# Two-pair partition moves, 64x64 tiles, 512-token FFN tiles and a shallower load queue in a fused attention and FFN kernel

## The chip, the cores and the metric

The kernel runs on one core of one Trainium2 chip. The metric is device time in microseconds (us), lower is better. The kernel before takes 254.39 us (median of 3 runs, 254.19 to 254.92). The span of a profile is about 1.8 us shorter than the time of the same run.

Engines are called as in the profile: PE (TensorE matmuls), PEld (its weight loads), DVE (VectorE), ACT (ScalarE), POOL (GpSimd, which issues the loads; before the change pair 0's q and k come through SP instead), SP (the sync engine, which issues stores and, after the change, moves; SPq in the profile is its queue). A matmul that runs at half clock is called cold here, one at full clock warm.

## The reference, cut to what matters

```
q, k, v: (8, 8, 576, 64) f32         # batch, heads, sequence, head size
chunks of 64 tokens; in each chunk and head:
    attn = softmax(q k^T / 8);  out = attn v
x = out, as (4608 tokens, 512)
result = ((x w1) * (x w2)) w3 w_out  # w1, w2: 512x1024; w3: 1024x1024; w_out: 1024x512
```

## The kernel before: the parts that matter here

The work is cut into 18 *pairs* of 256 tokens. A string lists every step in program order; each engine takes its own steps from it strictly in that order. For pair p:

- `q k v` load (POOL queue; casts f32 to bf16). `T p.s` transposes q or k blockwise (DVE). `S` computes scores (PE), `E` exponentials (ACT), `P` attention times v (PE), `N` divides (DVE), `X` transposes into xt (DVE).
- `A p.j`, `B p.j` are FFN matmuls with w1, w2 (PE), `C` copies A's result out of PSUM (ACT), `M` multiplies (DVE). `O` multiplies by w3 w_out (PE), `Y` copies (ACT) and stores (SP). `V W Z` form w3 w_out once. `D` is filler on zeros that keeps PE busy.

```
qk_t[p] = io.tile([P, 2, H, 2 * D], bf, tag="qk", bufs=6, name="qk")      # six pairs of q, k
vbuf = [consts.tile([P, 2, H, VW], bf, ...) for i in range(7)]            # seven pairs of v

def do_S(p):                       # 64 matmuls, K = 32 rows, accumulated over e
    for h in range(H):
        for e in range(2):
            for i in range(NB):    # NB = 4 blocks of 32 partitions
                mm(s_t[p][half[i % 2], i // 2, h * CH:(h + 1) * CH],
                   lhsT=qkT[blk[i], 1, e, h, :], rhs=qkT[blk[i], 0, e, h, :], start=(e == 0), stop=(e == 1))
def mm_ab(p, j, which):            # FFN: 256 tokens per matmul
    for i in range(2):
        for ki in range(KO):
            mm(ps_t[p, j][:, which, i * PT:(i + 1) * PT], lhsT=w[:, ki, ...], rhs=xt[:, ki, p * PT:(p + 1) * PT], ...)
...
S9 N8.0 O5 E9 X8.0 N8.1 X8.1 T11.0 A6.1 T11.1 Y5 B6.1 C6.1 ... P9 l16 M6.3 S10    # one pair's steps; l = q, k, v
```

All PSUM results share a ring of four buffers: a step that writes PSUM waits for the reader of the result four steps back.

The softmax here doesn't subtract the row's maximum and nothing guards it: scores larger than these inputs give would overflow.

Of the kernel before, what the change touches and what calls it, by code (L numbers as in the profile page):

```python
# [356 lines left out]
```

## Time and profile before

| Reading | Value | View |
|---|---|---|
| PE busy | 234.9 of 252.7 us (93%) | page, part 1 |
| One pair in steady state | 12.0 us | timeline of PE |
| of it A and B (64 matmuls of 256 columns) | 7.08 us, 110.6 ns each | timeline |
| O (16 of 512 columns) | 3.45 us, 215.6 ns each | timeline |
| P and S (64 small matmuls each) | 0.62 and 0.64 us, 9.9 ns each | timeline |
| DVE waiting for q, k loads | 3.5 us | waits |

The slices of the page: the span in 40 parts; each digit is the busy share in tenths (PEclk: the granted clock).

```profile
PE   1389999999899999999999999999999999999993
...
PEclk9999999999999999999999999999999999999999
DMA  7999999999999999999953020202021120102022
```

PE is full from 20 us to the end, so the kernel is bound by PE's own work. The DMA engines are full only for the first half.

The timeline of PE in steady state; the columns are start and duration in us, engine, line, operation, out<-in, the part of the array used (rows*columns), the shape of the moving operand, count. Durations overlap because matmuls are pipelined, so costs are read from start to start.

```profile
140.11 0.70 PE L88 MATMUL pv<-vbuf,e 64*32 64x65 bf16 x64
140.73 0.70 PE L88 MATMUL s_ps<-qkT 32*64 32x64 bf16 x64
141.57 3.61 PE L88 MATMUL o_ps<-w3o,ab 128*128 128x512 bf16 x16
145.02 7.15 PE L88 MATMUL ab_ps<-xt,w 128*128 128x256 bf16 x64
152.10 0.70 PE L88 MATMUL pv<-vbuf,e 64*32 64x65 bf16 x64
```

From 140.11 to 152.10 is one pair. O starts 0.20 us later than S's 0.64 us would allow: the chain of waits shows that it waits for the multiply of the last A, B (its PSUM buffer).

### The profile page before, as it was taken

The page shows a single profiled execution, that of the slowest core. Times are in us where ns is not written, and L with a number is a line of the kernel's source. Part 1 is how long each engine was busy: PE and PEld are TensorE (multiplying, and loading weights), DVE is VectorE, ACT ScalarE, POOL GpSimd, SP SyncE. Part 2 cuts the span into 40 slices and gives each one's busy share as a digit, 9 for nine tenths or more (in the row PEclk, how much of TensorE's full clock was granted, in tenths as well). Part 3 has the DMA queues.
Part 4 walks back from the last instruction along what each step waited for, and adds up shares of the span by engine and source line. Part 5 has one row for each costly group of instructions (what it writes and reads, how often), then busy time and mean ns, then how long its engine had stood idle before and what let it go on. Part 6 is the DMA issues. An engine that isn't in the chain of part 4 may idle for free.

```text
span 252.7 us, 8382 instructions
## 1 busy us (share of the span) xinstructions
PE 234.9 (93%) x3841; PEld 170.5 (67%) x3841; DVE 156.4 (62%) x233; ACT 86.3 (34%) x116; POOL 82.9 (33%) x110
## 2 busy tenths in 40 slices
PE   1389999999899999999999999999999999999993
PEld 1237878854555577866868686868686868678662
DVE  1665999699996457486665758584945445432230
ACT  3312424432433343333334243343334332323321
POOL 8756975657984567654020000000000000000000
PEclk9999999999999999999999999999999999999999
DMA  7999999999999999999953020202021120102022
GB/s 177 182 184 177 182 175 202 196 184 167 175 170 214 244 227 182 199 167 148 187 38 92 3 83 4 86 3 86 5 81 44 46 81 5 64 22 84 0 86 83
DMA packets 89763, 29.90 MB, mean 118 GB/s; under 512 B 73728, under 2 KB 85248, under 8 KB 89728
## 3 DMA queue, kind: packets, MB, share of 16 engines
q0 software_dynamic: 82592, 18.88, 80.4%
q1 hardware_dynamic: 7136, 10.49, 11.8%
q8 instruction: 30, 0.49, 0.7%
q14 instruction: 5, 0.04, 0.0%
HBM read 38.80 MB, written 9.44 MB: 191 GB/s over the span
## 4 chain that ended last, share of the span: by engine, by line
PE 65%; DMA 14%; DVE 10%; POOL 4%; ACT 3%; issue 3%; DVEq 0%; POOLq 0%
PE ab_ps L88 39%; PE o_ps L88 25%; DMA w<-in_moe_w_dram 4%; DVE ab L249 4%; DMA qk<-in_q_dram 4%; DMA qk<-in_k_dram 3%; DVE w3T L290 3%; DMA vbuf<-in_v_dram 3%; ACT a_sb L244 3%; POOL w L91 1%; DVE qkT L168 1%; POOL vbuf L91 1%; POOL qk L91 1%; POOL wo L91 1%; DVE xt L213 1%
## 5 line engine op out<-in xcount | busy, mean ns | idle before, releaser
L88 PE MATMUL ab_ps<-xt,w 128*128 128x256 bf16 x1136 | 128.0, 273 | 1.3 <-DVE xt L213 1.3
L88 PEld LDWEIGHTS <-w 128*128 128x128 bf16 x1152 | 112.3, 98 | 19.4 <-DVE xt L213 2.4
L249 DVE TENSOR_TENSOR ab<-a_sb,ab_ps 128x512 bf16<-128x512 f32 x71 | 48.3, 682 | 71.6 <-ACT a_sb L244 71.6
L244 ACT COPY a_sb<-ab_ps 128x512 f32<-128x512 f32 x71 | 41.6, 586 | 79.3 <-PE ab_ps L88 79.3
L88 PE MATMUL o_ps<-w3o,ab 128*128 128x512 bf16 (+1 forms) x296 | 65.3, 373 | 2.7 <-ACT o_sb L276 1.1
L88 PEld LDWEIGHTS <-ab 128*128 128x128 bf16 x296 | 28.7, 97 | 33.3 <-issue 1.6
L168 DVE STREAM_TRANSPOSE qkT<-qk 128x1024 bf16<-128x1024 bf16 x36 | 45.1, 1287 | 8.5 <-ACT qk L133 5.1
L91 POOL DMA_DIRECT2D vbuf<-in_v_dram x40 | 33.9, 852 | 31.3 <-PE pv L88 16.3
L283 ACT COPY o_sb<-o_ps 128x1024 f32<-128x1024 f32 x17 | 17.2, 1014 | 45.9 <-PE o_ps L88 43.2
L213 DVE STREAM_TRANSPOSE xt<-xn 128x512 bf16<-128x512 bf16 x36 | 25.6, 712 | 1.2
L209 DVE TENSOR_TENSOR xn<-pv,rc 128x512 bf16<-128x512 f32 x36 | 24.9, 692 | 1.2
L91 POOL DMA_DIRECT2D qk<-in_q_dram x23 | 18.1, 793 | 6.8 <-DMA qk<-in_k_dram 2.4
L184 ACT ACTIVATE e<-s_ps 128x1024 bf16<-128x1024 f32 x16 | 16.4, 1025 | 8.7 <-PE s_ps L88 8.4
...
L88 PEld LDWEIGHTS <-qkT 32*64 32x64 bf16 x1152 | 11.4, 111 | 10.6 <-DVE qkT L168 9.6
L88 PE MATMUL w_ps<-wo,w3T 128*128 128x512 bf16 x64 | 14.2, 379 | 0.0
L88 PEld LDWEIGHTS <-e 64*32 64x32 bf16 x1152 | 10.1, 90 | 5.5 <-issue 3.6
L88 PE MATMUL pv<-vbuf,e 64*32 64x65 bf16 x1152 | 12.7, 197 | 1.1 <-ACT e L184 1.1
L91 POOL DMA_DIRECT2D w<-in_moe_w_dram x16 | 11.1, 697 | 5.4 <-DMA wo<-in_moe_w_out_dram 3.0
L88 PE MATMUL s_ps<-qkT 32*64 32x64 bf16 x1024 | 11.3, 193 | 0.0
L88 PEld LDWEIGHTS <-w3T 128*128 128x128 bf16 x64 | 6.2, 98 | 7.1
L290 DVE STREAM_TRANSPOSE w3T<-w 128x1024 bf16<-128x1024 bf16 x8 | 9.6, 1211 | 0.9 <-DMA w<-in_moe_w_dram 0.9
...
## 6 DMA issues: line engine op xcount, KB each, us to landing
...
```

Of the source, the lines that this page charges most:

```text
L88: return inorder(nc.tensor.matmul(*a, **kw))
L91: return inorder(nc.gpsimd.dma_start(dst, src))
L168: inorder(nc.vector.transpose(qkT_t[p][:, s].rearrange("p e h (y t) -> p h t e y", t=2), qk_t[p][:, s].rearrange("p h (t e y) -> p h t e y ...
L184: inorder(nc.scalar.activation(e_t[p][:].rearrange("p u h q -> p u (h q)"), s_t.pop(p)[:], Exp, scale=scale, bias=0.0))
L209: inorder(nc.vector.tensor_mul(xn_t[p, u][:], pv[:, :, :, 0:D], rc.to_broadcast([P, 2, 4, D])))
L213: inorder(nc.vector.transpose(xt[:, :, t0:t0 + UT].rearrange("p o (m y) -> p m o y", y=BL), xn_t.pop((p, u))[:].rearrange("p r (c n) (z o) ...
L244: inorder(nc.scalar.copy(a_t[p, j][:], ps_t[p, j][:, 0, :]))
L249: inorder(nc.vector.tensor_mul(ab_t[p][:, 2 * j:2 * j + 2, :].rearrange("p j t -> p (j t)"), a_t.pop((p, j))[:], ps_t.pop((p, j))[:, 1, :]))
L283: inorder(nc.scalar.copy(o_sb[:], ps_t.pop(p)[:]))
L290: inorder(nc.vector.transpose(w3T_t[f][:].rearrange("p k (f y) -> p f k y", y=BL), w3[:, NB * f:NB * (f + 1), :].rearrange("p f (k x) -> p ...
```

## The change

From pair 8 on, q, k and x of *two pairs* at a time are moved between partitions by SBUF-to-SBUF DMAs (`G`, `H`, issued from SP). Then the contraction of S is 64 rows instead of twice 32, S and P run in 64x64 tiles with 32 matmuls each instead of 64, and the FFN takes 512 tokens per matmul instead of 256. To make room, and to leave the DMA engines free, loads are held: two buffers of q, k (two pairs ahead) and three of v. The order of all steps is new.

```
-    vbuf = [... for i in range(7)]
+    vbuf = [... for i in range(3)]
-            qk_t[p] = io.tile(..., tag="qk", bufs=6, ...)
+            qk_t[p] = io.tile(..., tag="qk", bufs=2, ...)
-            if p == 0:   # pair 0: f32 load on SP and a cast on ACT
-                ...
+    def do_G(g, a):                       # q, k of two pairs: 4 moves of 128 KB for each a = 0, 1
+        for i in (2 * a, 2 * a + 1):
+            for e in range(2):
+                move(qkm_t[g][blk[2 * a + e], i % 2], qkT_t[g][blk[i], e])
     def do_S(p):
+            if p < 8: (as before) else:
+                for i in (0, 3, 1, 2):
+                    mm(s_t[p][half[i % 2], i // 2, ...],
+                       lhsT=qkm_t[g][half[i // 2], i % 2, m, 1, h, :],
+                       rhs=qkm_t[g][half[i // 2], i % 2, m, 0, h, :], start=True, stop=True)
+    def do_H(g, a): ...                   # x of two pairs: 4 moves of 64 KB for each a
     do_P, do_X, do_A, do_B, do_M: likewise, two forms (p < 8 and p >= 8)
     do_O of the last pair: three PSUM tiles instead of one
+    do_Q: the store of O, apart from its copy Y
ORDER (start, and around pairs 8 to 12):
-l0 q1 i0 k1 v1 i1 i2 l2 i3 l3 l4 o h0 h1 l5 D0.0.16.64 ...
+q0 k0 v0 q1 k1 v1 i0 D0.0.104.64 T0.0 T0.1 q2 k2 v2 i1 i2 i3 S0 ...
-N6.1 X6.1 T9.0 T9.1 O3 ... P7 l14 M4.3 S8 N7.0 O4 ... T10.0 A5.0 T10.1 ... P8 l15 M6.0 S9 ... T11.0 ...
+T8.1 M4.2 T9.0 P6 v9 q10 k10 Y1 S7 T9.1 ... G4.0 ... O2 M4.3 N6.1 G4.1 X6.1 T10.0 P7 v10 q11 k11 ... O3 ...
+S8 Y3 A5.1 E8 B5.1 Q3 O4 ... T11.0 P8 v11 q12 k12 ... S9 ... A6.1 T12.0 B6.1 C6.1 M6.0 P9 v12 q13 k13 ...
-... A17.3 ... M17.3 O17 Y17
+... A16.7 ... M16.7 O16 O17 Y16 Q16 Y17 Q17
```

More of the change, by code (lines that the diff above doesn't have):

```diff
@@ L9 @@
 ORDER = """
-l0 q1 i0 k1 v1 i1 i2 l2 i3 l3 l4 o h0 h1 l5 D0.0.16.64 T0.0 T0.1 l6 S0 T1.0 E0 P0 D0.1.4.512 T1.1 l7
-N0.0 S1 D1.0.5.512 X0.0 N0.1 X0.1 A0.0 E1 B0.0 C0.0 P1 M0.0 A0.1 N1.0 X1.0 B0.1 C0.1 N1.1 A0.2 X1.1
-B0.2 C0.2 M0.1 A1.0 T2.0 B1.0 C1.0 M0.2 A1.1 T2.1 l8 B1.1 C1.1 M1.0 S2 M1.1 A0.3 E2 T3.0 B0.3 C0.3
-P2 M0.3 A1.2 N2.0 X2.0 B1.2 C1.2 N2.1 A1.3 X2.1 B1.3 C1.3 M1.2 A2.0 T3.1 l9 B2.0 C2.0 M1.3 S3 T4.0
-A2.1 E3 M2.0 B2.1 T4.1 C2.1 P3 l10 M2.1 A2.2 N3.0 B2.2 C2.2 X3.0 A2.3 N3.1 B2.3 X3.1 C2.3 M2.2 S4
@@ L15 @@
-M2.3 A3.0 E4 B3.0 C3.0 A3.1 M3.0 B3.1 C3.1 V0 A3.2 M3.1 B3.2 C3.2 V1 A3.3 M3.2 B3.3 C3.3 V2 W0 M3.3
-V3 T5.0 W1 Z0 V4 V5 T5.1 W2 Z1 V6 V7 T6.0 P4 l11 Z2 S5 T6.1 W3 E5 N4.0 X4.0 N4.1 X4.1 T7.0 A4.0 Z3
-B4.0 T7.1 C4.0 P5 l12 M4.0 S6 N5.0 O0 E6 X5.0 N5.1 X5.1 T8.0 O1 Y0 T8.1 P6 l13 Y1 S7 N6.0 O2 E7 X6.0
-N6.1 X6.1 T9.0 T9.1 O3 Y2 A4.1 Y3 B4.1 C4.1 A4.2 M4.1 B4.2 C4.2 A4.3 M4.2 B4.3 C4.3 P7 l14 M4.3 S8
-N7.0 O4 E8 X7.0 N7.1 X7.1 T10.0 A5.0 T10.1 Y4 B5.0 C5.0 A5.1 M5.0 B5.1 C5.1 A5.2 M5.1 B5.2 C5.2 A5.3
@@ L20 @@
-M5.2 B5.3 C5.3 A6.0 M5.3 B6.0 C6.0 P8 l15 M6.0 S9 N8.0 O5 E9 X8.0 N8.1 X8.1 T11.0 A6.1 T11.1 Y5 B6.1
-C6.1 A6.2 M6.1 B6.2 C6.2 A6.3 M6.2 B6.3 C6.3 P9 l16 M6.3 S10 N9.0 O6 E10 X9.0 N9.1 X9.1 T12.0 A7.0
-T12.1 Y6 B7.0 C7.0 A7.1 M7.0 B7.1 C7.1 A7.2 M7.1 B7.2 C7.2 A7.3 M7.2 B7.3 C7.3 P10 l17 M7.3 S11
-N10.0 O7 E11 X10.0 N10.1 X10.1 T13.0 A8.0 T13.1 Y7 B8.0 C8.0 A8.1 M8.0 B8.1 C8.1 A8.2 M8.1 B8.2 C8.2
-A8.3 M8.2 B8.3 C8.3 P11 M8.3 S12 N11.0 O8 E12 X11.0 N11.1 X11.1 T14.0 A9.0 T14.1 Y8 B9.0 C9.0 A9.1
@@ L25 @@
-M9.0 B9.1 C9.1 A9.2 M9.1 B9.2 C9.2 A9.3 M9.2 B9.3 C9.3 P12 M9.3 S13 N12.0 O9 E13 X12.0 N12.1 X12.1
-T15.0 A10.0 T15.1 Y9 B10.0 C10.0 A10.1 M10.0 B10.1 C10.1 A10.2 M10.1 B10.2 C10.2 A10.3 M10.2 B10.3
-C10.3 P13 M10.3 S14 N13.0 O10 E14 X13.0 N13.1 X13.1 T16.0 A11.0 T16.1 Y10 B11.0 C11.0 A11.1 M11.0
-B11.1 C11.1 A11.2 M11.1 B11.2 C11.2 A11.3 M11.2 B11.3 C11.3 P14 M11.3 S15 N14.0 O11 E15 X14.0 N14.1
-X14.1 T17.0 A12.0 T17.1 Y11 B12.0 C12.0 A12.1 M12.0 B12.1 C12.1 A12.2 M12.1 B12.2 C12.2 A12.3 M12.2
@@ L30 @@
-B12.3 C12.3 P15 M12.3 S16 N15.0 O12 E16 X15.0 N15.1 X15.1 A13.0 Y12 B13.0 C13.0 A13.1 M13.0 B13.1
-C13.1 A13.2 M13.1 B13.2 C13.2 A13.3 M13.2 B13.3 C13.3 P16 M13.3 S17 N16.0 O13 E17 X16.0 N16.1 X16.1
-A14.0 Y13 B14.0 C14.0 A14.1 M14.0 B14.1 C14.1 A14.2 M14.1 B14.2 C14.2 A14.3 M14.2 B14.3 C14.3 P17
-M14.3 A15.0 N17.0 X17.0 B15.0 C15.0 N17.1 O14 X17.1 M15.0 A15.1 Y14 B15.1 C15.1 A15.2 M15.1 B15.2
-C15.2 A15.3 M15.2 B15.3 C15.3 A16.0 M15.3 B16.0 C16.0 O15 M16.0 A16.1 Y15 B16.1 C16.1 A16.2 M16.1
-B16.2 C16.2 A16.3 M16.2 B16.3 C16.3 A17.0 M16.3 B17.0 C17.0 O16 M17.0 A17.1 Y16 B17.1 C17.1 A17.2
@@ L36 @@
-M17.1 B17.2 C17.2 A17.3 M17.2 B17.3 C17.3 M17.3 O17 Y17
+q0 k0 v0 q1 k1 v1 i0 D0.0.104.64 T0.0 T0.1 q2 k2 v2 i1 i2 i3 S0 E0 T1.0 P0 D0.1.4.512 T1.1 q3 k3 v3
+o h0 S1 N0.0 X0.0 E1 N0.1 P1 X0.1 T2.0 A0.0 T2.1 q4 k4 v4 h1 N1.0 B0.0 C0.0 X1.0 S2 M0.0 A0.1 E2
+N1.1 C0.1 B0.1 X1.1 A1.0 M0.1 B1.0 C1.0 P2 M1.0 A0.2 N2.0 B0.2 X2.0 C0.2 A0.3 N2.1 B0.3 X2.1 C0.3
+M0.2 A1.1 M0.3 B1.1 C1.1 T3.0 A1.2 M1.1 B1.2 C1.2 T3.1 q5 k5 v5 A1.3 B1.3 M1.2 C1.3 S3 M1.3 A2.0 E3
+B2.0 C2.0 A2.1 M2.0 B2.1 C2.1 P3 M2.1 A2.2 N3.0 B2.2 X3.0 C2.2 A2.3 N3.1 B2.3 X3.1 C2.3 M2.2 A3.0
@@ new lines @@
+M2.3 B3.0 C3.0 V0 A3.1 M3.0 B3.1 C3.1 V1 A3.2 M3.1 B3.2 C3.2 V2 W0 M3.2 V3 T4.0 W1 Z0 T4.1 q6 k6 v6
+V4 V5 S4 Z1 A3.3 V6 E4 B3.3 V7 C3.3 P4 W2 M3.3 N4.0 X4.0 N4.1 X4.1 W3 T5.0 Z2 T5.1 q7 k7 v7 T6.0 S5
+Z3 T6.1 q8 k8 A4.0 E5 B4.0 C4.0 P5 v8 M4.0 A4.1 N5.0 B4.1 C4.1 X5.0 O0 M4.1 N5.1 X5.1 T7.0 S6 Y0
+T7.1 q9 k9 A4.2 E6 Q0 B4.2 T8.0 C4.2 O1 T8.1 M4.2 T9.0 P6 v9 q10 k10 Y1 S7 T9.1 A4.3 Q1 E7 N6.0 G4.0
+B4.3 C4.3 X6.0 O2 M4.3 N6.1 G4.1 X6.1 T10.0 P7 v10 q11 k11 Y2 A5.0 T10.1 Q2 B5.0 C5.0 N7.0 O3 X7.0
@@ new lines @@
+M5.0 N7.1 X7.1 S8 Y3 A5.1 E8 B5.1 Q3 O4 C5.1 M5.1 T11.0 P8 v11 q12 k12 Y4 A5.2 T11.1 Q4 B5.2 C5.2
+N8.0 G5.0 A5.3 M5.2 B5.3 N8.1 C5.3 S9 X8.0 A6.0 G5.1 E9 X8.1 B6.0 M5.3 C6.0 A6.1 T12.0 B6.1 C6.1
+M6.0 P9 v12 q13 k13 M6.1 A6.2 N9.0 B6.2 C6.2 N9.1 O5 X9.0 X9.1 M6.2 H4.0 T12.1 A6.3 Y5 B6.3 H4.1
+C6.3 S10 M6.3 A7.0 E10 B7.0 C7.0 Q5 T13.0 P10 v13 q14 k14 A7.1 M7.0 B7.1 C7.1 N10.0 O6 M7.1 N10.1
+X10.0 X10.1 T13.1 A7.2 Y6 B7.2 C7.2 G6.0 A7.3 M7.2 B7.3 T14.0 C7.3 S11 A8.0 G6.1 M7.3 E11 T14.1 B8.0
+C8.0 P11 v14 q15 k15 M8.0 A8.1 Q6 N11.0 B8.1 C8.1 N11.1 O7 X11.0 X11.1 M8.1 H5.0 A8.2 Y7 B8.2 H5.1
@@ new lines @@
+C8.2 T15.0 A8.3 M8.2 B8.3 C8.3 T15.1 S12 Q7 A8.4 E12 M8.3 G7.0 B8.4 C8.4 P12 v15 q16 k16 M8.4 A8.5
+N12.0 B8.5 G7.1 C8.5 N12.1 A8.6 X12.0 B8.6 C8.6 X12.1 A8.7 M8.5 M8.6 B8.7 C8.7 S13 M8.7 A10.0 E13
+B10.0 C10.0 P13 v16 q17 k17 M10.0 A10.1 N13.0 B10.1 C10.1 N13.1 O8 X13.0 X13.1 M10.1 H6.0 T16.0 O9
+Y8 T16.1 H6.1 T17.0 T17.1 A10.2 Q8 Y9 B10.2 C10.2 G8.0 A10.3 M10.2 B10.3 C10.3 S14 M10.3 A10.4 G8.1
+E14 B10.4 C10.4 P14 v17 M10.4 A10.5 Q9 N14.0 B10.5 C10.5 N14.1 A10.6 X14.0 B10.6 C10.6 X14.1 A10.7
@@ new lines @@
+M10.5 M10.6 B10.7 C10.7 S15 M10.7 A12.0 E15 B12.0 C12.0 P15 M12.0 A12.1 N15.0 B12.1 C12.1 N15.1 O10
+X15.0 X15.1 M12.1 H7.0 O11 Y10 H7.1 A12.2 Q10 Y11 B12.2 C12.2 Q11 A12.3 M12.2 B12.3 C12.3 S16 M12.3
+A12.4 E16 B12.4 C12.4 P16 M12.4 A12.5 N16.0 B12.5 C12.5 N16.1 A12.6 X16.0 B12.6 C12.6 X16.1 A12.7
+M12.5 M12.6 B12.7 C12.7 S17 M12.7 A14.0 E17 B14.0 C14.0 P17 M14.0 A14.1 N17.0 B14.1 C14.1 N17.1 O12
+X17.0 X17.1 M14.1 H8.0 O13 Y12 H8.1 A14.2 Q12 Y13 B14.2 C14.2 Q13 A14.3 M14.2 B14.3 C14.3 A14.4
+M14.3 B14.4 C14.4 A14.5 M14.4 B14.5 C14.5 A14.6 M14.5 B14.6 C14.6 A14.7 M14.6 B14.7 C14.7 A16.0
@@ L37 @@
+M14.7 B16.0 C16.0 O14 M16.0 O15 Y14 Q14 A16.1 Y15 B16.1 C16.1 Q15 A16.2 M16.1 B16.2 C16.2 A16.3
+M16.2 B16.3 C16.3 A16.4 M16.3 B16.4 C16.4 A16.5 M16.4 B16.5 C16.5 A16.6 M16.5 B16.6 C16.6 A16.7
+M16.6 B16.7 C16.7 M16.7 O16 O17 Y16 Q16 Y17 Q17
 """
@@ L66 @@
     PT = 2 * UT
+    GT = 2 * PT
     NP = NT // PT
@@ L102 @@
     w3o = wpool.tile([P, FO, DM], bf, name="w3o")
-    xt = wpool.tile([P, KO, NT], bf, name="xt")
     zero = consts.tile([P, 512], bf, name="zero")
     inorder(nc.vector.memset(zero[:], 0.0))
-    vbuf = [consts.tile([P, 2, H, VW], bf, name=f"vbuf{i}") for i in range(7)]
+    vbuf = [consts.tile([P, 2, H, VW], bf, name=f"vbuf{i}") for i in range(3)]
     for t in vbuf:
@@ L125, in load_qk @@
         if p not in qk_t:
-            qk_t[p] = io.tile([P, 2, H, 2 * D], bf, tag="qk", bufs=6, name="qk")
+            qk_t[p] = io.tile([P, 2, H, 2 * D], bf, tag="qk", bufs=2, name="qk")
         for s in which:
-            if p == 0:
-                raw = io.tile([P, H, 2 * D], f32, tag="raw", name="raw")
-                inorder(nc.sync.dma_start(
-                    raw[:], (q, k)[s][0, :, 0:4 * CH, :].rearrange("h (p t) d -> p h (t d)", t=2)))
-                inorder(nc.scalar.copy(qk_t[p][:, s], raw[:]))
-                continue
             for at, b, c, m in spans(4 * p, 4):
@@ L141, in load_v @@
             for at, b, c, m in spans(4 * p + 2 * u, 2):
-                load(vbuf[p % 7][at * CH:(at + m) * CH, u, :, 0:D],
+                load(vbuf[p % 3][at * CH:(at + m) * CH, u, :, 0:D],
                      v[b, :, c * CH:(c + m) * CH, :].rearrange("h p d -> p h d"))
@@ L160, with move @@
     blk = [slice(i * BL, (i + 1) * BL) for i in range(NB)]
-    qkT_t, s_t, e_t, pv_t, xn_t = {}, {}, {}, {}, {}
+    qkT_t, qkm_t, s_t, e_t, pv_t, xn_t, xm_t, xt_t = {}, {}, {}, {}, {}, {}, {}, {}
+    def move(dst, src):
+        inorder(nc.sync.dma_start(dst, src))
     def do_T(p, s):
-        if s == 0:
-            qkT_t[p] = asb.tile([P, 2, 2, H, CH], bf, tag="qkT", bufs=2, name="qkT")
+        g = p // 2
+        if g not in qkT_t:
+            qkT_t[g] = asb.tile([P, 2, 2, 2, H, CH], bf, tag="qkT", bufs=2, name="qkT")
         inorder(nc.vector.transpose(
-            qkT_t[p][:, s].rearrange("p e h (y t) -> p h t e y", t=2),
+            qkT_t[g][:, :, p % 2, s].rearrange("p e h (y t) -> p h t e y", t=2),
             qk_t[p][:, s].rearrange("p h (t e y) -> p h t e y", t=2, e=2)))
+    def do_G(g, a):
+        if a == 0:
+            qkm_t[g] = asb.tile([P, 2, 2, 2, H, CH], bf, tag="qkm", bufs=2, name="qkm")
+        for i in (2 * a, 2 * a + 1):
+            for e in range(2):
+                move(qkm_t[g][blk[2 * a + e], i % 2], qkT_t[g][blk[i], e])
     def do_S(p):
-        qkT = qkT_t.pop(p)
+        g, m = divmod(p, 2)
         s_t[p] = s_t.pop(p) if p in s_t else psum("s_ps")
         for h in range(H):
-            for e in range(2):
-                for i in range(NB):
+            if p < 8:
+                for e in range(2):
+                    for i in range(NB):
+                        mm(s_t[p][half[i % 2], i // 2, h * CH:(h + 1) * CH],
+                           lhsT=qkT_t[g][blk[i], e, m, 1, h, :], rhs=qkT_t[g][blk[i], e, m, 0, h, :],
+                           start=(e == 0), stop=(e == 1))
+            else:
+                for i in (0, 3, 1, 2):
                     mm(s_t[p][half[i % 2], i // 2, h * CH:(h + 1) * CH],
-                       lhsT=qkT[blk[i], 1, e, h, :],
-                       rhs=qkT[blk[i], 0, e, h, :], start=(e == 0), stop=(e == 1))
+                       lhsT=qkm_t[g][half[i // 2], i % 2, m, 1, h, :],
+                       rhs=qkm_t[g][half[i // 2], i % 2, m, 0, h, :], start=True, stop=True)
     def do_E(p):
@@ L186, in do_E, with do_P @@
             Exp, scale=scale, bias=0.0))
-    def do_P(p, u):
-        e = e_t[p] if u == 0 else e_t.pop(p)
-        pv = pv_t[p, u] = psum("pv")
-        for n in range(2):
-            for qh in range(2):
-                for g in range(NB):
-                    for r in range(2):
-                        at = (2 * qh + n) * W
-                        mm(pv[blk[g], r, at:at + W],
-                           lhsT=e[half[r], u, 2 * g + n, qh * BL:(qh + 1) * BL],
-                           rhs=vbuf[p % 7][half[r], u, 2 * g + n, 0:W], start=True, stop=True)
-    def do_P2(p):
-        do_P(p, 0)
-        do_P(p, 1)
+    def do_P(p):
+        e = e_t.pop(p)
+        for u in range(2):
+            pv = pv_t[p, u] = psum("pv")
+            for m in range(4):
+                if p < 8:
+                    for g in range(NB):
+                        for r in range(2):
+                            mm(pv[blk[g], r, m * W:(m + 1) * W],
+                               lhsT=e[half[r], u, 2 * g + m % 2, m // 2 * BL:(m // 2 + 1) * BL],
+                               rhs=vbuf[p % 3][half[r], u, 2 * g + m % 2, 0:W], start=True, stop=True)
+                else:
+                    for g, r in ((0, 0), (1, 1), (1, 0), (0, 1)):
+                        mm(pv[half[g], r, m * W:(m + 1) * W], lhsT=e[half[r], u, 4 * g + m, :],
+                           rhs=vbuf[p % 3][half[r], u, 4 * g + m, 0:W], start=True, stop=True)
     def do_N(p, u):
@@ L207, in do_N, with new_xt, do_H @@
         inorder(nc.vector.reciprocal(rc[:], pv[:, :, :, D:W]))
-        xn_t[p, u] = asb.tile([P, 2, 4, D], bf, tag="xn", bufs=2, name="xn")
-        inorder(nc.vector.tensor_mul(xn_t[p, u][:], pv[:, :, :, 0:D], rc.to_broadcast([P, 2, 4, D])))
-    def do_X(p, u):
-        t0 = p * PT + u * UT
-        inorder(nc.vector.transpose(
-            xt[:, :, t0:t0 + UT].rearrange("p o (m y) -> p m o y", y=BL),
-            xn_t.pop((p, u))[:].rearrange("p r (c n) (z o) -> p (r c) o n z", c=2, o=KO)))
-    ab_t, ps_t, a_t = {}, {}, {}
+        if u == 0:
+            xn_t[p] = asb.tile([P, 2, 2, 4, D], bf, tag="xn", bufs=3, name="xn")
+        inorder(nc.vector.tensor_mul(xn_t[p][:, u], pv[:, :, :, 0:D], rc.to_broadcast([P, 2, 4, D])))
+    def new_xt(g):
+        if g not in xt_t:
+            xt_t[g] = asb.tile([P, KO * GT], bf, tag="xt", bufs=4, name="xt")
+        return xt_t[g]
+    def do_X(p, u):
+        g, m = divmod(p, 2)
+        if p < 8:
+            t0 = m * PT + u * UT
+            inorder(nc.vector.transpose(
+                new_xt(g)[:].rearrange("p (o t) -> p o t", o=KO)[:, :, t0:t0 + UT]
+                .rearrange("p o (m y) -> p m o y", y=BL),
+                xn_t[p][:, u].rearrange("p r (c n) (z o) -> p (r c) o n z", c=2, o=KO)))
+        else:
+            if g not in xm_t:
+                xm_t[g] = asb.tile([P, 2, KO, 2, UT], bf, tag="xm", bufs=2, name="xm")
+            inorder(nc.vector.transpose(
+                xm_t[g][:, u, :, m].rearrange("p o (c y) -> p c o y", y=BL),
+                xn_t[p][:].rearrange("p u r m d -> p (u r) m d")[:, :, 2 * u:2 * u + 2]
+                .rearrange("p c n (z o) -> p c o n z", o=KO)))
+    def do_H(g, a):
+        xt = new_xt(g)[:].rearrange("p (s c) -> p s c", s=2)
+        for k_ in range(2):
+            for i in (2 * a, 2 * a + 1):
+                move(xt[blk[2 * a + k_], i % 2], xm_t[g][blk[i], k_].rearrange("p o m t -> p (o m t)"))
+    ab_t, ps_t, a_t, o_t = {}, {}, {}, {}
     def do_D(which, p, n, cols):
@@ L225, in do_D, with do_AB @@
             mm(d[key][:, 0, 0:cols], lhsT=zero[:, 0:P], rhs=zero[:, 0:cols], start=True, stop=True)
-    def mm_ab(p, j, which):
-        w = (w1, w2)[which]
-        for i in range(2):
+    def do_AB(p, j, f, which):
+        if p >= 8:
+            rhs = new_xt(p // 2)[:].rearrange("p (s o t) -> p o s t", s=2, o=KO)
+        else:
+            rhs = new_xt(p // 2)[:].rearrange("p (o t) -> p o t", o=KO)[:, :, p % 2 * PT:(p % 2 + 1) * PT]
+        fs = (f,) if p >= 8 else (2 * j, 2 * j + 1)
+        n = GT // len(fs)
+        for i, f in enumerate(fs):
             for ki in range(KO):
-                mm(ps_t[p, j][:, which, i * PT:(i + 1) * PT],
-                   lhsT=w[:, ki, (2 * j + i) * P:(2 * j + i + 1) * P],
-                   rhs=xt[:, ki, p * PT:(p + 1) * PT], start=(ki == 0), stop=(ki == KO - 1))
+                mm(ps_t[p, j][:, which, i * n:(i + 1) * n],
+                   lhsT=(w1, w2)[which][:, ki, f * P:(f + 1) * P], rhs=rhs[:, ki],
+                   start=(ki == 0), stop=(ki == KO - 1))
     def do_A(p, j):
         ps_t[p, j] = ps_t.pop((p, j)) if (p, j) in ps_t else psum("ab_ps")
-        mm_ab(p, j, 0)
+        do_AB(p, j, j, 0)
     def do_B(p, j):
-        mm_ab(p, j, 1)
+        do_AB(p, j, j, 1)
     def do_C(p, j):
@@ L246, in do_M, with mm_o @@
     def do_M(p, j):
-        if p not in ab_t:
-            ab_t[p] = msb.tile([P, FO, PT], bf, tag="ab", bufs=7, name="ab")
-        inorder(nc.vector.tensor_mul(
-            ab_t[p][:, 2 * j:2 * j + 2, :].rearrange("p j t -> p (j t)"), a_t.pop((p, j))[:],
-            ps_t.pop((p, j))[:, 1, :]))
+        g = p // 2
+        if g not in ab_t:
+            ab_t[g] = msb.tile([P, FO, GT], bf, tag="ab", bufs=4, name="ab")
+        if p < 8:
+            o = ab_t[g][:, 2 * j:2 * j + 2, p % 2 * PT:(p % 2 + 1) * PT]
+            view = lambda t: t.rearrange("p (j t) -> p j t", j=2)
+        else:
+            o = ab_t[g][:, j].rearrange("p (c s y) -> p s c y", s=2, y=BL)
+            view = lambda t: t.rearrange("p (s c y) -> p s c y", s=2, y=BL)
+        inorder(nc.vector.tensor_mul(o, view(a_t.pop((p, j))[:]), view(ps_t.pop((p, j))[:, 1, :])))
     def store(p, u0, u1, n0, n1, o_sb):
-        inorder(nc.sync.dma_start(
-            out[p * PT + u0 * UT:p * PT + u1 * UT, n0:n1].rearrange("(u p) n -> p u n", p=UT),
-            o_sb[:, u0:u1, n0:n1]))
-    def mm_o(p, u, n0, n1):
+        move(out[p * PT + u0 * UT:p * PT + u1 * UT, n0:n1].rearrange("(u p) n -> p u n", p=UT), o_sb)
+    def mm_o(dst, p, u, n0, n1):
         for ki in range(FO):
-            mm(ps_t[p][:, u, n0:n1], lhsT=ab_t[p][:, ki, u * UT:(u + 1) * UT],
+            t0 = p % 2 * PT + u * UT
+            mm(dst, lhsT=ab_t[p // 2][:, ki, t0:t0 + UT],
                rhs=w3o[:, ki, n0:n1], start=(ki == 0), stop=(ki == FO - 1))
     def do_O(p):
-        ps_t[p] = psum("o_ps")
         if p < NP - 1:
+            ps_t[p] = psum("o_ps")
             for u in range(2):
-                mm_o(p, u, 0, DM)
-            del ab_t[p]
+                mm_o(ps_t[p][:, u, :], p, u, 0, DM)
             return
-        t = ps_t[p]
         o_sb = msb.tile([P, 2, DM], f32, tag="o_sb", name="o_sb")
@@ L274, in do_O @@
                                 (1, DM // 2, DM, nc.vector.tensor_copy)):
-            mm_o(p, u, n0, n1)
-            inorder(copy(o_sb[:, u, n0:n1], t[:, u, n0:n1]))
-            store(p, u, u + 1, n0, n1, o_sb)
+            t = psum("o_ps")
+            mm_o(t[:, 0, 0:n1 - n0], p, u, n0, n1)
+            inorder(copy(o_sb[:, u, n0:n1], t[:, 0, 0:n1 - n0]))
+            store(p, u, u + 1, n0, n1, o_sb[:, u:u + 1, n0:n1])
     def do_Y(p):
@@ L283, in do_Y, with do_Q @@
         inorder(nc.scalar.copy(o_sb[:], ps_t.pop(p)[:]))
-        store(p, 0, 2, 0, DM, o_sb)
+        o_t[p] = o_sb
+    def do_Q(p):
+        if p < NP - 1:
+            store(p, 0, 2, 0, DM, o_t.pop(p)[:])
     w3T_t = {}
@@ L316, in load_half3 @@
         load_w3(i * n, (i + 1) * n)
-    do = {"l": load_pair, "q": lambda p: load_qk(p, (0,)), "k": lambda p: load_qk(p, (1,)), "v": load_v, "i": load_w12, "o": load_wo, "h": load_half3, "T": do_T, "S": do_S, "E": do_E,
-          "P": do_P2, "N": do_N, "X": do_X, "A": do_A, "B": do_B, "C": do_C, "M": do_M, "D": do_D, "V": do_V,
-          "W": do_W, "Z": do_Z, "O": do_O, "Y": do_Y}
+    do = {"l": load_pair, "q": lambda p: load_qk(p, (0,)), "k": lambda p: load_qk(p, (1,)), "v": load_v, "i": load_w12, "o": load_wo, "h": load_half3, "T": do_T, "S": do_S, "E": do_E, "G": do_G, "H": do_H,
+          "P": do_P, "N": do_N, "X": do_X, "A": do_A, "B": do_B, "C": do_C, "M": do_M, "D": do_D, "V": do_V,
+          "W": do_W, "Z": do_Z, "O": do_O, "Y": do_Y, "Q": do_Q}
     for step in ORDER.split():
```

## The prediction

> **What bounds the kernel now.** TensorE's own work. The page gives PE 93% busy; the stage table (ten-microsecond windows) gives 9.3 to 10.0 us of PE in every window from 20 to 240 us, at clock 1.00. Loads keep the DMA engines 80 to 100% busy until about 125 us, but after 20 us they cost PE almost nothing (three waits for xt, 1.3 us). The timeline shows a steady period of 12.0 us per pair, for example 140.11 to 152.10:
> - P (64 small matmuls) 0.62 us, S (64) 0.64 us, about 9.9 ns each whatever the tile shape;
> - 0.20 us until O starts: the chain of waits runs last ab matmul, a_sb copy (0.59), ab multiply (0.70), O, because O's PSUM buffer waits for that multiply; P and S lie inside this wait;
> - O 16 x 215.6 ns = 3.45 us; A and B 64 x 110.6 ns = 7.08 us.
>
> **What the change removes, adds, moves.**
> 1. FFN tiles of 512 tokens in pairs 8 to 17: two 256-column matmuls (221.2 ns) become one of 512 (215.6 ns). 320 x 5.6 ns = 1.8 us saved, all on PE. The Trainium skill, "TensorE: Matmul & The Clock Gate", section "Wait — 56ns, not 53.3ns?", gives N / 2.4 GHz plus about 2.5 ns; the trace agrees roughly (+4.0 and +2.3).
> 2. 64x64 tiles: P and S need 32 matmuls each instead of 64. The skill, "TensorEngine Tiling (Array Packing)", section "Tiling Modes", says that 64x64 gives four independent tiles, against eight here before. If 9.9 ns is an issue rate, each falls to 0.32 us; if four tiles don't hide weight loads, to about 0.45. I take 0.38: 1.26 becomes 0.76 us, 10 pairs, 5.0 us saved.
> 3. The new order puts A and B matmuls between multiply and the reuse of its PSUM buffer: the 0.20 us goes, 10 times, 2.0 us.
> 4. The last O uses separate PSUM tiles: the two PE waits for ACT o_sb (0.67 + 0.46) go, 1.1 us.
> 5. Added: 16 SBUF moves per two pairs on the sync queue (8 of 128 KB, 8 of 64 KB; about 7.9 MB in all, at some 0.4 us per issue as the stores show). They are issued many matmuls before use. I expect them off the chain; DVE work is unchanged (about 17 us per two pairs of about 22).
> 6. Start: q0 and k0 no longer wait for an f32 load and two ACT casts (1.05 us each), so S0 should start near 8 us instead of 9.4. But the second quarter of w1, w2 now comes after pair 2: at the 360 GB/s of f32 reads that the windows show (180 GB/s written, half the bytes) it lands near 22 us, where the old kernel started A0.1 at 21.3. Net about zero.
> 7. Loads held back: loads now wait for transposes and P, and run to the end. Some T will arrive late around pairs 8 and 9; I allow 1.5 us of new PE waits.
>
> **Sum.** 252.7 us span - 1.8 - 5.0 - 2.0 - 1.1 + 1.5 = 244.3; plus 1.8 us between span and time: **246.2 us**, 80% range 242.0 to 251.0. Faster by over 2%: 0.75; within 2%: 0.22; slower: 0.03.
>
> **What would show it.** Period of a pair after pair 8 near 11.2 us; P and S of 32 matmuls 0.32 to 0.45 us from start to next start; A/B 215.6 ns per 512 columns; no 0.2 us before O; PE idle for DMA moves near zero; ab/o chain with PE above 70%.
>
> **What would make it wrong.** 64x64 matmuls taking 20 ns each (item 2 gone, about 251); S waiting for moves behind queued loads or stores; PE starving at 15 to 30 us for w1, w2; DVE stalled by late q, k near pairs 8 to 10 and dragging PE.

## More of the kernel before

Waits: who waited for whom; total us, times, longest.

```profile
POOL vbuf L91 <- PE pv L88: 16.3, 3, 8.5
DVE qkT L168 <- DMA qk<-in_k_dram: 2.8, 1, 2.8
DVE qkT L168 <- DMA qk<-in_q_dram: 0.7, 2, 0.4
```

DVE hardly ever waits for q or k.

## The result, and the profile after

The changed kernel takes 268.38 us (4 runs, 267.04 to 270.71) against 254.4 us; the ratio is 1.056 (95% interval 1.048 to 1.063). It is 5.6% slower. Executions over 1.5% slower than the fastest of the same kernel are left out of the means. Ratios are the mean time of one kernel's runs over that of the other's of the same rounds, so they are not quite the ratio of the medians quoted.

The same slices after:

```profile
PE   7567999999999777985999978999999999999992
...
PEclk9658999999999995996899999999999999999998
DMA  8999999999799999299879999994925006004004
```

The last third is as full as before. The loss lies in the holes of the PE row at 80 to 100, 120 and 155 us, and in the clock: in the stage table (windows of 10 us) it is 0.50 at 10 to 20 us, and 0.66 at 100 to 110 and at 120 to 130 us. In the stage table PE is busy 147.2 us of the 160 us from 80 to 240 us; before it was 158.7.

The steady state, once loads are done, is what was predicted in kind:

```profile
177.36 3.62 PE L92 MATMUL ab_ps<-xt,w 128*128 128x512 bf16 x16
180.91 0.45 PE L92 MATMUL s_ps<-qkm 64*64 64x64 bf16 x32
181.29 1.90 PE L92 MATMUL ab_ps<-xt,w 128*128 128x512 bf16 x8
183.12 0.45 PE L92 MATMUL pv<-vbuf,e 64*64 64x65 bf16 x32
183.50 5.35 PE L92 MATMUL ab_ps<-xt,w 128*128 128x512 bf16 x24
188.78 0.45 PE L92 MATMUL s_ps<-qkm 64*64 64x64 bf16 x32
```

S takes 0.38 us from its start to the next (180.91 to 181.29), P 0.38 us, and a 512-column matmul 215.7 ns (56 of them from 222.95 to 235.03 us). From S at 165.99 to S at 188.78, two pairs take 22.79 us, or 11.4 us a pair.

Waits after:

```profile
POOL vbuf L95 <- PE pv L92: 71.0, 10, 13.4
DVE qkT L171 <- DMA qk<-in_q_dram: 25.4, 9, 4.5
POOL qk L95 <- DVE qkT L171: 15.7, 3, 6.5
DVE qkT L171 <- DMA qk<-in_k_dram: 4.5, 5, 2.3
```

POOL now waits 71 us for P instead of 16.3, and DVE waits 30 us for q and k instead of 3.5. Of these 30 us, 9.0 lie before 22 us, in the new start, and stay in v5qk6 and best (8.9 and 8.7); the 20.9 us after 78 us are what the hold can explain. One link of the loop, from three timelines (PE, POOL, DVE; pair 12 is the one whose q is loaded at 112.95):

```profile
110.11 0.45 PE L92 MATMUL pv<-vbuf,e 64*64 64x65 bf16 x32
118.06 0.45 PE L92 MATMUL pv<-vbuf,e 64*64 64x65 bf16 x32
122.89 3.57 PE L92 MATMUL ab_ps<-xt,w 128*128 128x256 bf16 x16 [4.39 <-DVE ab L306]
```

```profile
110.74 2.25 POOL L95 DMA_DIRECT2D vbuf<-in_v_dram  x3 [13.37 <-PE pv L92]
112.95 0.92 POOL L95 DMA_DIRECT2D qk<-in_q_dram  x1
```

```profile
120.98 1.31 DVE L171 STREAM_TRANSPOSE qkT<-qk 128x1024 bf16<-128x1024 bf16 x1 [4.48 <-DMA qk<-in_q_dram]
122.19 1.25 DVE L306 TENSOR_TENSOR ab<-a_sb,ab_ps 128x512 bf16<-128x512 f32 x2
```

The numbers in brackets are the idle time just before and its releaser. POOL stood 13.37 us at the load of v11, which waits for P8 (its buffer is v8's); P8 runs at 110.11. Only then can POOL issue v11 and, behind it, q12 and k12, although q12's own buffer had been free for 11 us: it was pair 10's, and T10.1 had read it by 99.4 us (start 98.07, 1.32 long). T12 on DVE waits 4.48 us for q12, until 120.98; behind T12 stand the multiplies (122.19); PE waits 4.39 us for one of them. And then the FFN runs cold: 16 matmuls of 256 columns take 3.37 us (122.89 to 126.26) instead of 1.77. PE is late, so the next P is late, and so the next load. The waits of PE from 80 to 165 us (2.51, 2.16, 0.83, 4.39, 2.48) sum to 12.4 us (in the timeline of DVE all but the 0.83, which is for a move, follow a wait for q or k), and the cold matmuls at 101 to 110 and 122 to 131 us cost, against their warm durations, 5.7 us more.

The Trainium skill, "TensorE: Matmul & The Clock Gate", Part 1, says that an idle PE falls back from 2.4 to 1.2 GHz. The trace agrees: 3.37 us / 16 = 211 ns for 256 columns is half speed. Not every stall is followed by it: after the wait of 2.51 us the 16 matmuls of O took 3.56 us, near their warm 3.45.

### The profile page after: what moved, and what is told of

It reads as the page before. It is cut to its first block, busy times and chain, and to the rows that moved or that the text cites. A ratio compares the mean times of both kernels' runs of the same rounds, so it can differ in the third digit from the quotient of the medians.

```text
span 266.1 us, 6804 instructions
## 1 busy us (share of the span) xinstructions
PE 239.3 (90%) x2964; PEld 139.8 (53%) x2964; DVE 154.8 (58%) x229; ACT 82.8 (31%) x114; POOL 84.4 (32%) x112
## 4 chain that ended last, share of the span: by engine, by line
PE 53%; issue 16%; DMA 12%; POOL 9%; DVE 5%; SPq 1%; ACT 1%; POOLq 0%
PE ab_ps L92 31%; PE o_ps L92 14%; DMA qk<-in_k_dram 5%; PE w_ps L92 5%; DMA w<-in_moe_w_dram 5%; POOL qk L95 5%; POOL vbuf L95 4%; DVE qkT L171 2%; PE pv L92 2%; DMA qkm<-qkT 2%; SPq L163 1%; PE s_ps L92 1%; DVE xn L229 1%; DVE xt L241 1%; DVE ab L306 1%
## 5 line engine op out<-in xcount | busy, mean ns | idle before, releaser
L92 PE MATMUL ab_ps<-xt,w 128*128 128x256 bf16 (+1 forms) x832 | 136.8, 322 | 6.4 <-DVE ab L306 4.4
L92 PEld LDWEIGHTS <-w 128*128 128x128 bf16 x832 | 81.1, 100 | 51.0 <-issue 5.4
L92 PE MATMUL o_ps<-w3o,ab 128*128 128x512 bf16 (+1 forms) x296 | 66.3, 381 | 2.5 <-DVE xn L229 2.5
L171 DVE STREAM_TRANSPOSE qkT<-qk 128x1024 bf16<-128x1024 bf16 x36 | 46.3, 1302 | 30.4 <-DMA qk<-in_q_dram 25.4
L95 POOL DMA_DIRECT2D qk<-in_q_dram x24 | 19.1, 799 | 18.3 <-DVE qkT L171 15.7
L92 PE MATMUL pv<-vbuf,e 64*32 64x65 bf16 (+1 forms) x832 | 10.7, 201 | 5.4 <-DVE ab L306 2.5
L92 PEld LDWEIGHTS <-e 64*32 64x32 bf16 (+1 forms) x832 | 8.2, 98 | 11.6 <-issue 8.9
L249 DVE STREAM_TRANSPOSE xm<-xn 128x512 bf16<-128x512 bf16 x20 | 13.0, 690 | 0.4
L241 DVE STREAM_TRANSPOSE xt<-xn 128x512 bf16<-128x512 bf16 x16 | 11.4, 711 | 0.5
L92 PEld LDWEIGHTS <-qkT 32*64 32x64 bf16 x512 | 5.7, 120 | 6.4 <-DVE qkT L171 4.9
```

The costliest lines, as they stand in the source:

```text
L92: return inorder(nc.tensor.matmul(*a, **kw))
L95: return inorder(nc.gpsimd.dma_start(dst, src))
L171: inorder(nc.vector.transpose(qkT_t[g][:, :, p % 2, s].rearrange("p e h (y t) -> p h t e y", t=2), qk_t[p][:, s].rearrange("p h (t e y) -> ...
L241: inorder(nc.vector.transpose(new_xt(g)[:].rearrange("p (o t) -> p o t", o=KO)[:, :, t0:t0 + UT] .rearrange("p o (m y) -> p m o y", y=BL), ...
L249: inorder(nc.vector.transpose(xm_t[g][:, u, :, m].rearrange("p o (c y) -> p c o y", y=BL), xn_t[p][:].rearrange("p u r m d -> p (u r) m d" ...
```

## The experiments

Theory A: the in-order queue of load issues. v of pair p+3 waits there for P of pair p, and q, k stand behind it. Rivals: B, the two buffers of q, k themselves; C, moves and loads contend on the DMA engines. The first four runs change only buffers or only the order of issues.

**v5**: `range(3)` becomes `range(5)` for vbuf (and `p % 3` becomes `p % 5`).

> The changed kernel with five buffers of v instead of three, q and k still two; the order is untouched. Theory A (the queue of load issues is in order: v of pair p+3 waits there for P of pair p, and q, k of the pair after stand behind it and come late): the waits of the load queue for P (71 us) fall below 15 us, DVE waits for q, k (30 us) fall below 8 us, no window falls to half clock, time 245 to 251 us. Theory B (the two buffers of q, k are what holds loads): little changes, 263 to 268. Theory C (moves and loads contend on the DMA engines): no gain, or worse, about 268.

Measured: 255.77 us (255.65 to 256.68), ratio to the kernel before 1.005. The load queue's waits for P vanish from the view; what is left of the waits for q:

```profile
DVE qkT L171 <- DMA qk<-in_q_dram: 12.1, 4, 4.2
```

Five more kilobytes per partition give 12.6 us back. Of the 12.1 us of waits for q, 9.3 are those of the start; after it one of 2.8 us is left, at pair 9. The direction is A's; the time is 5 us above A's range, and the window from 90 to 100 us was still partly cold (clock 0.84).

**qk4**: `tag="qk", bufs=2` becomes 4.

> The changed kernel with four buffers of q, k, v still three. Theory A: q, k still stand in the queue behind v, so the gain is small: 262 to 268 us, the load queue still waits 60 us or more for P. Theory B: most of the loss comes back, 245 to 252 us. Theory C: about 268.

Measured: 272.1 us (270.78 to 273.08). So theory B falls as the main cause: deeper buffers behind a blocked queue bring nothing; POOL waited 87.7 us for P. That it is even slower than the changed kernel is a miss of A's range. Its PE waits 5.98 and 8.18 us at pairs 8 and 12; why these grew is not settled. A small part of B is true. The first wait of PE in the changed kernel goes back to q9, which stood behind nothing but its own buffer, until T7.1 had read it:

```profile
79.04 0.88 POOL L95 DMA_DIRECT2D qk<-in_q_dram  x1 [4.02 <-DVE qkT L171]
84.82 1.32 DVE L171 STREAM_TRANSPOSE qkT<-qk 128x1024 bf16<-128x1024 bf16 x1 [2.56 <-DMA qk<-in_q_dram]
88.46 3.63 PE L92 MATMUL o_ps<-w3o,ab 128*128 128x512 bf16 x16 [2.51 <-DVE xn L229]
```

That wait of PE is gone in qk4 and v5qk6; v5 keeps it (2.36 us, with partly cold matmuls of O behind it).

**v5qk6**: both deeper (v five, q, k six).

> The changed kernel with five buffers of v and six of q, k: loads are no longer held, nothing else changes. If holding loads is the whole cause (A and B together): 244 to 249 us, as the blind sum without its late loads had it. Theory C: loads now saturate the DMA engines to about 125 us beside the moves, so moves arrive late and PE waits for qkm and xt: over 255 us.

Measured: 256.13 us (254.86 to 257.35), ratio 1.006. No better than v5: some 9 us remain above the range, so holding is not the whole cause. After 22 us DVE no longer waits for q or k at all. Theory C, as stated (over 255 us, PE waiting for qkm), fits in part. The line below is S of pair 8, its first matmul apart; it waits 2.86 us for a move, and it runs cold after that:

```profile
96.54 0.21 PE L92 MATMUL s_ps<-qkm 64*64 64x64 bf16 x1
99.61 0.93 PE L92 MATMUL s_ps<-qkm 64*64 64x64 bf16 x31 [2.86 <-DMA qkm<-qkT]
100.48 3.60 PE L92 MATMUL ab_ps<-xt,w 128*128 128x256 bf16 x16
```

SP's timeline and the view of the moves explain it. The last transpose of pair 9 ends at 85.3 us; the eight moves are issued in 6.95 us (issue of all eight, first start to last end; median 0.59 us each, where I took 0.4), and they land 2.5 to 9.1 us later (median 4.8) beside the loads:

```profile
85.58 6.95 SPq L163 DMA_DIRECT2D qkm<-qkT  x8
```

From the transpose to S is 14 us. So the time that the moves take is real, but it costs PE 2.86 us in one place, the first group of moves, and only 0.49 us at another. That loads slow the moves is not isolated: the first two groups land after a median of 8.3 and 8.4 us, the third after 3.5, although the DMA row still shows 9 there.

**fifo_first**: the buffers of the change (two and three); q, k of pairs 10 to 17 issued right after the transposes that free their buffer.

```
-T8.1 M4.2 T9.0 P6 v9 q10 k10 ... T10.1 ... P8 v11 q12 k12 ...
+T8.1 q10 k10 M4.2 T9.0 P6 v9 ... T10.1 q12 k12 ... P8 v11 ...
```

> The changed kernel with the same two and three buffers; only the place of q, k loads from pair 10 on in the order of load issues changes: right after the transposes that free their buffer, ahead of the v load that waits for P. Theory A: q, k no longer stand behind v, so half or more of the 14 us over the kernel before comes back: 250 to 258 us (the stalls at pairs 8 and 9 before the edit stay). Theory B (buffer count alone): 265 to 268.

Measured: 255.94 us (253.66 to 257.84), ratio 1.001 from its three fast runs; the run of 257.84 is slow. The same gain as v5 without a byte of memory. With qk4 this settles A against B: what mattered most was what q, k stood behind.

The second batch of runs starts from v5qk6 and takes on what was left.

**s8late**: S of pair 8 after O4 instead of before A5.1.

```
-S8 Y3 A5.1 E8 B5.1 Q3 O4 C5.1 M5.1 T11.0 P8 ...
+Y3 A5.1 B5.1 Q3 C5.1 O4 M5.1 S8 Y4 T11.0 A5.2 E8 B5.2 C5.2 P8 ...
```

> Run v5qk6 with S of pair 8 placed after O4 instead of before A5.1, 5.2 us more PE work before it. If the moves' own delay (14 us from the last transpose of pair 9 to the last landing) costs a 2.9 us PE stall and the half clock that follows it: PE waits for qkm near zero, window 100 to 110 us at clock 1.0, 3.5 to 6 us less than v5qk6, about 251. If that stall is slack that comes back elsewhere: no change.

Measured: 249.01 us (248.83 to 250.3), ratio 0.979 (0.977 to 0.981): faster than the kernel before by 2.1%, so whether by 2% is just unclear, and 2.7% (1.006 - 0.979, about 6.9 us) better than v5qk6. PE no longer waits for a move:

```profile
98.24 3.62 PE L92 MATMUL o_ps<-w3o,ab 128*128 128x512 bf16 x16
101.79 0.44 PE L92 MATMUL s_ps<-qkm 64*64 64x64 bf16 x32
102.17 1.92 PE L92 MATMUL ab_ps<-xt,w 128*128 128x256 bf16 x16
```

The trace of v5qk6 gives about 6.5 us to this: 3.6 us of waits for moves and issue in 96 to 125 us, and 2.9 us of cold matmuls.

**tail**: `O16 O17 Y16 Q16` becomes `O16 Y16 Q16 O17`.

> Run v5qk6 with the last steps reordered: the copy and the 512 KB store of O16 come before O17 instead of after it. If the late store of O16 is what keeps the end at 4.9 us after the last matmul (3.3 us in the kernel before): 1.2 to 2 us less than v5qk6, near 254.4. If the end is set by the last small store: no change.

Measured: 252.63 us (250.72 to 253.52), ratio 0.992, 3.6 us under v5qk6. That is more than the edit can do: in the two profiles, PE's last O already starts 3.3 us apart (243.55 and 240.25), before the edited place. Both kernels stall at pair 8, and their times spread by 2.5 us (v5qk6) and 2.8 us (tail) from run to run. So this run alone does not size the edit; run best does it better.

**start**: the beginning in the order of the kernel before, up to A2.0, with loads `q0 k0 v0 q1 i0 k1 v1 i1 i2 q2 ...` and the second filler.

> Run v5qk6 with the beginning in the order of the kernel before (w1, w2 quarters ahead of pair 2, the second filler, A0 and A1 ahead of S2), up to A2.0. If the new start costs the 2.5 to 3.3 us read from the timelines at P2: about 253 and clock above 0.9 in 10 to 30 us. If it is made up later: no change.

Measured: 258.85 us (258.51 to 259.76), ratio 1.017. A miss, and not a faithful undoing: the old order relied on the separate f32 load of pair 0 on SP, which I left out. Without it S1 starts at 16.73 us instead of 14.19, and the clock at 10 to 20 us is no better (0.52).

**all3**: the three together.

> The three edits together on v5qk6. If the blind sum was right once its three false terms are mended: 246 to 249 us, more than 2% faster than the kernel before. If the losses overlap or come back: 250 to 253.

Measured: 251.84 us (250.49 to 252.42), ratio 0.989, the start's loss included.

**best**: v5qk6 with s8late and tail.

> Run v5qk6 with the two edits that paid (O16 stored before O17; S of pair 8 after O4), without the edit of the start. If the two add: 249.0 minus 1.5 to 2.5, so 246.5 to 247.5, near the blind sum. If the 3.6 us of run tail was mostly the spread of the start: 248.5 to 249.5.

Measured: 248.71 us (248.66 to 249.25), ratio 0.976 (0.975 to 0.978). This beats both kernels. Against s8late the tail edit brings 0.7 us by the ratios (0.979 - 0.976) and 0.3 us by the medians; in the profiles the last O starts at 236.46 and 236.38 us, and the spans are 248.5 and 246.9. So the edit is worth something between 0.3 and 1.6 us; as the profile of s8late is of its slowest run (250.3, the other three 248.8 to 249.2), the lower figure is the likelier, and less than expected. The slices of best:

```profile
PE   8557899999999999999999999999999999999994
...
PEclk9857899999999999999999999999999999999999
DMA  7999999999999999999999996392061016004004
```

The holes are gone although the DMA row is now full to 150 us.

**best_start2**: another start (second quarter of w1, w2 right after the first; A0.1 and A1.0 before S2; two filler matmuls after S1).

> Run best with another start: the second quarter of w1, w2 right after the first, A0.1 and A1.0 before S2, and a filler of two matmuls after S1 to keep the clock up. If late w1, w2 and half clock from 11 to 25 us cost 1.5 to 3 us: 244 to 246, clock in 20 to 30 us near 1.0. If pair 2 now comes as much later as the weights came earlier: same as best.

Measured: 248.64 us (248.12 to 249.07), ratio 0.975, the same as best. S of pair 2 starts at 27.31 us instead of 21.54, while the FFN step that had waited for weights no longer does; W starts at 52.09 instead of 52.45.

**no_moves**: best without G and H; S, P and X in the old form everywhere, FFN tiles of 512 kept (`rhs` reads 512 tokens of an xt that X filled directly).

> Run best without any move: S, P in 32-row tiles and X straight into xt in all pairs, FFN tiles of 512 kept. P and S then cost about 1.26 us of PE a pair again instead of 0.76: 10 x 0.5 = 5 us more than best, near 251.5 to 252.5. If the moves cost as much as the 64x64 tiles bring (contention, sync queue): the same as best.

Measured: 252.83 us (251.96 to 254.88), ratio 0.993. The 64x64 tiles with all their moves are worth 1.7% (0.993 - 0.976), about 4.3 us, close to the 5 us predicted for them. The four runs spread by 2.9 us, but the profiles agree: from the first W to the last O, PE takes 188.4 us here and 183.9 in best. The 512-token tiles need no move at all.

So far: lifting the hold helps the changed kernel by 12.6 us. Does holding hurt the kernel before too?

**hold_before**: the kernel before with `bufs=6` to 2 and `range(7)` to 3, and its loads issued as the change issues them (v10, q11, k11 after P7 where l14 stood); all other steps stay in their order.

> The kernel before with its loads held as in the change: q, k two buffers, v three, the same order of load issues, nothing else. If holding loads alone is what hurts: 3 to 14 us slower than the kernel before, DVE waits for q, k of 10 us or more, PE idle above 5 us between 20 and 240 us. If holding hurts only together with moves and 64x64 tiles: within 1 us of the kernel before.

Measured: 254.38 us (254.32 to 254.64), ratio 0.998. No loss at all, though POOL stands as long as in the changed kernel:

```profile
POOL vbuf L92 <- PE pv L89: 74.8, 11, 10.0
DVE qkT L169 <- DMA qk<-in_k_dram: 2.8, 1, 2.8
DVE qkT L169 <- DMA qk<-in_q_dram: 1.5, 3, 0.9
```

So my theory A was incomplete: a blocked load queue costs nothing by itself. DVE hardly waits (4.3 us against 3.5). Theory D: the hold hurts where the consumer of the load also moved earlier. In hold_before, q12 is issued behind P8 at 109.00 us, and T12 stands after P9 and starts at 120.78, 11.8 us later, without a wait. In the change, q12 is issued after P8 and T12 stands before P9, which PE reaches 8.0 us later (110.11 to 118.06); but from P8 to the start of T12 the load needs 10.9 us (110.11 to 120.98): 2.8 until q is issued behind v, 8.0 until it has landed. T moved up because two pairs are moved at once.

**early_T** and **early_T_hold**: the kernel before, no moves; each T from pair 8 on one pair earlier, with a third qkT buffer; without and with the hold.

```
-P8 l15 M6.0 S9 N8.0 O5 E9 X8.0 N8.1 X8.1 T11.0 A6.1 T11.1
+P8 l15 M6.0 S9 N8.0 O5 E9 X8.0 N8.1 X8.1 T12.0 A6.1 T12.1
```

> The kernel before with its deep load buffers; only the transposes of q, k from pair 8 on stand one pair earlier in the order of DVE (a third qkT buffer holds the result), as moving two pairs at a time requires. Theory D (a held load hurts only where its consumer also moved earlier, so each factor alone is free): within 0.5% of the kernel before, 253.5 to 256. If early transposes hurt by themselves, because DVE serves FFN multiplies late: 257 or more.

Measured: 257.21 us (256.14 to 258.3), ratio 1.011. Not free: T8 now stands on DVE before a multiply of pair 4, and the profile has O0 waiting 2.06 us for that multiply.

> Both factors in the kernel before: transposes one pair earlier as in early_T, loads held as in hold_before (two buffers of q, k, three of v, v ahead of q, k in the queue). No move, no 64x64 tile, no 512-token tile. Theory D: q, k of pair p+4 are issued after P of pair p and wanted about 4 us later but need about 8 to 10 us, so DVE waits 4 to 6 us a pair, and PE goes cold now and then: 262 to 280 us. If it is the moves that hold loads up: as the kernel before, under 257.

Measured: 261.11 us (260.35 to 261.85), ratio 1.027.

```profile
POOL vbuf L92 <- PE pv L89: 79.8, 12, 10.0
DVE qkT L169 <- DMA qk<-in_q_dram: 32.3, 11, 6.9
DVE qkT L169 <- DMA qk<-in_k_dram: 4.5, 4, 2.8
```

| kernel before with | loads free | loads held |
|---|---|---|
| T as it was | 1 | 0.998 |
| T one pair earlier | 1.011 | 1.027 |

If the two factors were independent, both together would give 0.998 x 1.011 = 1.009. The other 1.8%, about 4.6 us, is their interaction, and DVE's wait for q and k is back (36.8 us). D is shown in direction, in the kernel before; in the changed kernel, where the moves need the early T, it could not be switched off. In size it falls short of my range and of the 12.6 us in the changed kernel. One difference between the two is visible: the clock of early_T_hold is 0.997, its longest single PE wait after 60 us 2.6 us, and the 256-column matmuls behind its waits keep their 110.6 ns, so PE does not go cold; in the changed kernel the stalls are longer and cold matmuls add 5.7 us. That this and the different place of the steps make up the rest is argued, not shown.

**best_fifo**: best with the two and three buffers, cured by order alone as in fifo_first.

> The edits of run best, but with the two and three buffers of the change: q, k of pairs 10 to 17 stand ahead of v in the load queue. If the depth of the buffers was never what was needed: 248 to 250.5 us. If depth counts, at pairs 8 and 9 above all, where the order cannot help: 251 to 254.

Measured: 250.72 us (249.56 to 251.75), ratio 0.985. It is between the two expectations' ranges: order alone brings most of it, depth another 0.9%. At pair 9 DVE still waits 3.0 us for q, and PE 2.5 us behind it, a wait that best has not; this is the part of B named under qk4.

## Why the prediction was wrong, point by point

The prediction said 246.2 us and faster; it was 268.4 us and slower.

1. *FFN tiles of 512 tokens, 1.8 us*: right. 215.7 ns per 512 columns. The Trainium skill, "TensorE: Matmul & The Clock Gate", "Wait — 56ns, not 53.3ns?", gives about 2.5 ns of fixed cost per matmul; the trace has 2.4 ns here (215.7 - 512 / 2.4).
2. *64x64 tiles, 5.0 us*: right. 0.38 us for S and for P as assumed. All in all the tiles and their moves bring 4.3 us (no_moves).
3. *The 0.20 us before O goes, 2.0 us*: wrong in effect. A two-pair period is 22.79 us; 64 x 215.6 ns + 32 x 215.6 ns + 4 x 0.38 us = 22.22 us. So 0.57 us, 0.28 us a pair, is lost elsewhere: P and S now stand apart, and four of the FFN blocks between them take about 0.1 us more than their matmuls, one S 0.15 us more. The Trainium skill, "TensorEngine Tiling (Array Packing)", Key Properties, says that a change of tiling mode drains the engine; these gaps fit that, but no run isolates it.
4. *Separate PSUM tiles at the end, 1.1 us*: right on PE (the two waits are gone), but the copy and store of O16 were put behind O17. In v5qk6's profile 4.9 us pass between PE's end (250.7) and the end of the span, against 3.3 before.
5. *Moves off the chain*: wrong once, and the second largest loss. The first group needs 14 us from transpose to S; s8late got 6.9 us back by giving it time. My 0.4 us per issue was read from stores; moves took 0.59.
6. *Start, net zero*: slightly wrong. When W starts (51.27 us; before 52.25), the change has done one A, B step and one S less, 2.4 us of PE work, so it is 1.4 us behind.
7. *Loads held back, 1.5 us*: this is the step that failed most. The waits of PE at 80 to 165 us were 12.4 us and the half clock behind them cost 5.7 us more. I named the risk ("DVE stalled by late q, k near pairs 8 to 10 and dragging PE") but priced it as one late load. I checked whether each load was *free* to be issued in time. I did not follow the queue it stands in, nor see that the two-pair moves take one pair off the lead. Nor did I count that a PE stall of some microseconds is paid twice, the second time by the clock.

As a sum over the predicted span of 244.3 us: 16.6 (item 7, less the 1.5 allowed; one stall of item 5 is in it) + 1.7 (item 3, for the six pairs whose P and S stand among 512-token tiles) + 1.6 (item 4, estimated from the two ends) + 1.4 (item 6) = 21.3 us. The profile shows 21.8.

The experiments divide it otherwise, because in the changed kernel the stalls of items 5 and 7 overlap at pair 8. Lifting the hold gives 12.3 us (v5qk6) to 12.6 (v5), time for the first moves 6.9 (s8late), the tail 0.3 or a little more. That leads to 248.7 us (best), 2.5 above the prediction, about what items 3 and 6 add up to (3.1). So of the whole miss somewhat over 12 us belong to item 7 and about 7 to item 5.

## What to carry to other kernels

Before holding loads back, count for each load the time from the last thing its issue *queue* waits for to the first step that needs it, on every in-order engine in between; a queue that stood for 75 us cost nothing in one order of steps, and lifting one that stood for 71 us gave 12.6 us in another, where a consumer had moved up by one pair (with nothing else changed, in early_T_hold, the two together cost 4.6 us beyond what each costs alone). If a load is late, look first at what stands in front of it in the queue: reordering the issues gave here what 5 KB of buffers per partition gave. And price stalls of TensorE of some microseconds above their length: here 12.4 us of waits cost 5.7 us more in cold matmuls, though not every wait did.

## What the Trainium skill lacked or had wrong

- "TensorEngine Tiling (Array Packing)": it has about 60 cycles of overhead per matmul, and no rate for tiles that overlap ("TensorE: Matmul & The Clock Gate", Part 3, has one: starts about 4 ns apart). Here small matmuls start every 9.9 ns in 64x32 and 32x64 tiles and every 11.9 ns (0.38 us / 32) in 64x64 tiles. For the drain at a change of mode it has no figure. If all of the 0.57 us over two pairs were the drain of their eight changes, that would be about 0.07 us each, an estimate from item 3; what of it lies within the 0.38 us of S and P is not seen.
- "DMA: Bandwidth & Descriptors": no figure for the issue of an SBUF-to-SBUF move from the sync engine: 0.51 to 1.67 us, median 0.59, so eight moves hold the queue for 5 to 7 us. Its fit of 2.0 us + bytes / 436e3, made for GpSimd's path, gives an estimate of 2.3 us for 128 KB; the fastest move landed in 2.3 us, the median in 5.6, the slowest in 9.7.
- "TensorE: Matmul & The Clock Gate": it names an idle window of about 3.4 us for the fall to half clock. Here a single wait of 2.86 us was enough (v5qk6: 16 matmuls of 256 columns in 3.39 us), while after one of 2.57 us (early_T_hold, before O at 74.45 us) the matmuls stayed warm. In v5qk6 four waits of 0.9 to 1.1 us between 10 and 22 us went with half speed (clock 0.51 and 0.81 in the windows of 10 to 20 and 20 to 30 us).
- The same page warns that clock records are unreliable: in the kernel before the profile's page shows full clock from the start, while four 512-column fillers at 12.3 us had their weights loaded 0.43 us apart (12.70 and 13.13), which is half speed.
- No page puts a price on waiting issues in one load queue that hold up free ones behind them: qk4 and fifo_first, 272.1 and 255.9 us, show it.
